# Loading the second head pair's q and k in f32 through ScalarE's DMA queue, with the cast on GpSimd

## The chip, the cores and the metric

The kernel runs on one core of a Trainium2 chip. A core has TensorE (PE, matrix products and transposes), VectorE (DVE), ScalarE (ACT) and GpSimd (POOL), and SyncE (SP), which here only issues transfers. Transfers between the chip's main memory (HBM) and the on-chip SBUF run on 16 DMA engines that all queues share. The metric is the device time of one execution in microseconds (us); the number given for the kernel is the median of several runs.

## What is computed

The reference is a causal attention whose heads are of two kinds, followed by a soft mixture of experts with slots. All inputs and the output are f32.

```python
# q, k, v: (4, 8, 768, 64); retrieval heads see all earlier positions,
# the others only 4 sink positions and a window of 64
scores = q @ k.T / sqrt(64);  scores = where(mask, scores, -1e9)
a = exp(scores - max);        a = a / sum(a)
x = (a @ v)  rearranged to (3072, 512)
# soft mixture of experts: 8 experts, 4 slots each, phi (512, 32)
logits = x @ phi
d = softmax(logits, axis=0);  slot_input = d.T @ x
slot_out[e] = relu(slot_input[e] @ w1[e]) @ w2[e]     # w1 (8,512,1024), w2 (8,1024,512)
c = softmax(logits, axis=1);  out = c @ slot_out      # (3072, 512)
```

## The kernel before, in words

The 32 pairs of batch and head are worked off as 16 head pairs, n = 0 to 15. For one pair the loop (`for n in range(NP)`) does six chunks of scores on TensorE (`scores`, L174), each followed by an exponential on ScalarE (L187) that writes the transposed probabilities `pT` in bf16; a mask multiplication on VectorE (`mask`, L189); and, one pair later, the products with v (`pvmm`, L201) and the division by the row sum (`norm`, L211). q and k must first be transposed: `transposes` (L147) does this on TensorE from the bf16 tile `raws`, and `evac` (L156) copies the result to SBUF, q on VectorE (L165), k on ScalarE (L167). The transposes for a pair are placed within the loop step before it; those for the second pair (n = 1) stand at the end of step 0, behind its sixth chunk.

The order on every engine is the order of the source (`tc.manual_schedule()`); each engine and each queue works its instructions in that order, and waits are put between engines where data or a buffer demands them.

There are three DMA queues in use. GpSimd's queue takes nearly all loads. It reads f32 from HBM and writes bf16 into SBUF, so it casts on the way: `load_four` (L121) brings q and k for four heads, `load_v` (L125) brings v for four heads, `w_load` (L138) and later lines bring the expert weights. In step 0 and 1 of the loop it issues, in this order: q and k of the second four heads, the first expert's w1, the second v, q and k of the third four, the third v, and then weights as they come due. ScalarE's queue takes one thing only: the first pair's q and k, in f32, into the tile `stage` (L264 to L266). From there VectorE casts q (L293) and ScalarE casts k (L294) into the first half of `raws[0]`. SyncE's queue takes a 64-byte input, and the output at the end.

The second pair's q and k are the other half of `raws[0]`. `load_pair(1)` (L270) brings them by GpSimd's queue, as its first two transfers, ahead of an iota (L272) that VectorE needs for the identity matrix and the masks, and of the first v (L274).

Before the loop, TensorE runs 12 matrix products on zeros (`keep_busy`, L285) and then the first pair's transposes. VectorE builds the mask tiles (L295 to L322) between the casts and the first mask multiplication.

The tile `stage` is taken from the pool `ptp`, which has two buffers and serves the probabilities `pT` in turn. The pool `raw` has three buffers of q and k for four heads each.

After the loop, the last weights are loaded, the slots are summed, and the experts are computed: first products L534, second products L573 and `second` (L561, its matrix product on L565). The second products of the last expert are made in two halves, left and right, as their weights arrive; then the output is formed (L589 to L599) and stored.

Of the kernel before, what the change touches and what calls it, by code (L numbers as in the profile page):

```python
# [10 lines left out]
F32 = mybir.dt.float32  # L11
# [27 lines left out]
def kernel(  # L39
# [13 lines left out]
    nc = tc.nc  # L53
    P = 128
    B, H, S, D = q.shape
# [12 lines left out]
    ptp = ent(tc.tile_pool(name="ptp", bufs=2))  # L68
# [6 lines left out]
    def single(shape, dt, name, tag=None):  # L75
        return singles.tile(shape, dt, name=name, tag=tag or name)
# [23 lines left out]
    raws, TT, vf, pT, pv, xb = {}, {}, {}, {}, {}, {}  # L100
# [7 lines left out]
    def features(x, n):  # L108
        if n < 2:
            return x[:, :, :256].rearrange("p i (x g d) -> p i g x d", x=2, g=2)[:, :, n]  # L110
        return x[:, :, 128 * (n % 4):128 * (n % 4) + 128].rearrange("p i (h d) -> p i h d", h=2)

    def load_pair(n, order="qk"):
        for which in order:
            src, z = (q, 0) if which == "q" else (k, 1)
            nc.gpsimd.dma_start(raws[0][:, z, n * S:(n + 1) * S],
                                src[0, 2 * n:2 * n + 2].rearrange("h (p s) d -> (h p) (s d)", s=12))

    def load_four(m):
        b, h = m // 2, 4 * (m % 2)  # L120
        raws[m] = raw.tile([P, 2, 2 * S], BF16, tag="raw", name="raw")  # L121
        for z, src in enumerate((q, k)):
            nc.gpsimd.dma_start(raws[m][:, z], src[b, h:h + 4].rearrange("h (p s) d -> (h p) (s d)", s=24))

    def load_v(m):  # L125
        b, h = m // 2, 4 * (m % 2)
        nc.gpsimd.dma_start(vbs[m % 3].rearrange("p h j d -> p (h j) d")[:, :, :D],  # L127
                            v[b, h:h + 4].rearrange("h (j p) d -> p (h j) d", p=P))
# [9 lines left out]
    def w_load(upto):  # L138
        while wi[0] < min(upto, 2 * NE - 3):
            e = wi[0] % NE  # L140
            dst, src = ((w1s, w1v), (w2s, w2v))[wi[0] // NE]

            for p0, p1 in ((0, 112), (112, 117), (117, 122), (122, 127), (127, P)) if wi[0] == NE else ((0, P),):
                nc.gpsimd.dma_start(dst[e][p0:p1], src[e][p0:p1])  # L144
            wi[0] += 1
# [28 lines left out]
    def scores(n, c):  # L174
        o, ln, parts = CHUNKS[c]
        sc = scp.tile([P, 2, 512], F32, tag="sc", name="sc")
        at = 0
        kT, qT = TT[n // 2, "k"][:, n % 2], TT[n // 2, "q"][:, n % 2]
        for j, i0, cnt in parts:
            for hh in range(2):  # L180
                po = 64 * hh
                nc.tensor.matmul(sc[:, hh, at:at + 128 * cnt], kT[po:po + 64, j * 128:(j + 1) * 128],  # L182
                                 qT[po:po + 64, i0 * 128:(i0 + cnt) * 128], start=True, stop=True)
            at += 128 * cnt
        if c == 0:
            pT[n] = ptp.tile([P, 2, NPT], BF16, tag="pT", name="pT")
        nc.scalar.activation(pT[n][:, :, o:o + ln], sc[:, :, :ln], ACT.Exp, scale=scale)  # L187
# [13 lines left out]
    def pvmm(n, i):  # L201
        if i % 3 == 0:
            pv[n] = pvp.tile([P, 3, 2, 65], F32, tag="pv", name="pv")
        for hh in range(2):
            for j in range(i + 1):
                vv = vb(n) if i - j <= 1 else vf[n]
                o = BLK[j, i]
                nc.tensor.matmul(pv[n][:, i % 3, hh, :], pT[n][:, hh, o:o + 128], vv[:, hh, j, :D + 1],  # L208
                                 start=(j == 0), stop=(j == i))

    def norm(n, half):  # L211
        b, h = n // 4, 2 * (n % 4)
        if h == 0 and half == 0:
            xb[b] = xp.tile([P, 6, DM], BF16, tag="xb", name="xb")
        rs = small.tile([P, 3, 2, 1], F32, tag="rs", name="rs")
        nc.vector.reciprocal(rs, pv[n][:, :, :, 64:65])  # L216
        nc.vector.tensor_mul(  # L217
            features(xb[b][:, 3 * half:3 * half + 3], n),
            pv[n][:, :, :, :64], rs.to_broadcast([P, 3, 2, 64]))
# [10 lines left out]
    def logits_mm(b, dbs):  # L230
        if b not in lgs:
            lgs[b] = trp.tile([P, 256], F32, tag="tr", name="lg")
        for db in dbs:
            for g in range(3):
                nc.tensor.matmul(lgs[b][32 * g:32 * g + 32, :], phi[:, db], xT[:, db, 256 * g:256 * (g + 1)],  # L235
                                 start=(db == 0), stop=(db == 3))

    def logits_exp(b):
        nc.scalar.activation(expT[:, b], lgs[b][:96], ACT.Exp, accum_out=colpart[:, b:b + 1])  # L239
# [21 lines left out]
            nc.vector.tensor_add(slot_acc, slot_acc, sp)  # L261


    stage = ptp.tile([P, 2, S], F32, tag="pT", name="stage")  # L264
    for src, z in ((k, 1), (q, 0)):
        nc.scalar.dma_start(stage[:, z], src[0, 0:2].rearrange("h (p s) d -> (h p) (s d)", s=12))  # L266
    ir32 = is_retrieval.tensor.reshape([H]).bitcast(I32)
    nc.sync.dma_start(ri, bass.AP(tensor=ir32, offset=0, ap=[[0, 1], [1, 2 * H]]))
    raws[0] = raw.tile([P, 2, 2 * S], BF16, tag="raw", name="raw")
    load_pair(1)  # L270
    diff = single([P, 256], F32, "diff", tag="slot_acc")
    nc.gpsimd.iota(diff, pattern=[[1, 256]], base=0, channel_multiplier=-1,  # L272
                   allow_small_or_imprecise_dtypes=True)
    load_v(0)  # L274

    V = nc.vector
    zero = single([P, 512], BF16, "zero")
# [2 lines left out]
    def keep_busy(t, count):  # L280
        for _ in range(count):
            nc.tensor.matmul(t, zero[:, :P], zero, start=True, stop=True)  # L282
# [7 lines left out]
    sk2 = single([P, 1], F32, "sk2")  # L290
    ge = single([P, 256], BF16, "ge", tag="slot_bf")
    grade = single([P, 640], BF16, "grade", tag="expT")
    V.tensor_copy(raws[0][:, 0, :S], stage[:, 0])  # L293
    nc.scalar.copy(raws[0][:, 1, :S], stage[:, 1])  # L294
    V.tensor_single_scalar(ge, diff, 0.0, op=ALU.is_ge)  # L295
    V.tensor_single_scalar(rne, ri.rearrange("p (h c) -> p h c", c=2), 0.0, op=ALU.not_equal)
    V.tensor_tensor(rrow1, rne[:, :, 0], rne[:, :, 1], op=ALU.max)
# [43 lines left out]
    for n in range(NP):  # L341
        if n == 0:
            load_four(1)
            nc.gpsimd.dma_start(w1s[0], w1v[0])
            load_v(1)
        elif n == 1:
            load_four(2)
            load_v(2)
        elif n % 2 == 0 and n < 12:
            load_four(n // 2 + 2)  # L350
        elif n % 2 == 1 and n < 12:
            load_v((n + 3) // 2)
        w_load(1 + 5 * (n + 1) // 8)
        if n == 3:
            for a in range(2):
                for g in range(2):
                    nc.gpsimd.dma_start(phi[64 * g:64 * g + 64, 2 * a:2 * a + 2],
                                        moe_phi.rearrange("(a g x d) s -> a g d x s", a=2, g=2, x=2)[a, g])

        m, x = (1, 0) if n == 1 else (n // 2 + 1, n % 2)  # L360
        turns = 0 < n < NP - 2
        b, r = n // 4 - 1, n % 4
        last = n - 1

        scores(n, 0)
        if n == 0:
            keep_busy(idle, 1)
        if n >= 1:
            for i in range(3):
                pvmm(last, i)  # L370
        if b >= 0 and r == 2:
            logits_mm(b, (0, 1, 2, 3))

        scores(n, 1)
        if n == 0:
            keep_busy(idle, 1)
        if b >= 0 and r == 2:
            logits_exp(b)
        if n >= 1:
            norm(last, 0)  # L380
        if turns:
            evac(m, x, "q", transposes(m, x, "q"))
        mask(n, 0)
        if b >= 0 and r == 3:
            exp_tokens(b)

        scores(n, 2)
        if n == 0:
            keep_busy(idle, 1)
        if n >= 1:  # L390
            pvmm(last, 3)
        if n == 3:
            x_transpose(0)
        if n >= 3:
            x_transpose(n - 2)
        mask(n, 1)

        scores(n, 3)
        if n == 0:
            keep_busy(idle, 1)  # L400
        if turns:
            tk = transposes(m, x, "k")

        scores(n, 4)
        if n == 0:
            keep_busy(idle, 1)
        if turns:
            evac(m, x, "k", tk)
        if n >= 1:
            pvmm(last, 4)  # L410
        mask(n, 2)
        if n:
            vfar(n)

        scores(n, 5)
        if n == 0:
            vfar(0)
        if n >= 1:
            pvmm(last, 5)
            norm(last, 1)  # L420
        if b >= 0 and r == 3:
            dispatch_mm(b)
            slot_sum(b)
        if n < 2:
            for which in ("q", "k"):
                evac(n, 1, which, transposes(n, 1, which))
        if n < 3:
            far_mask(n + 1)
            for h in range(H)[heads(n + 1)]:
                head_mask(h)  # L430
        elif n == 3:
            setup_late()

            expT = single([96, B, 256], BF16, "expT")
            slot_acc = single([P, DM], F32, "slot_acc")
            slot_bf = single([P, DM], BF16, "slot_bf")
# [232 lines left out]
```

## Time and profile before

| What | Value |
|---|---|
| Median of 5 runs | 154.42 us (153.55 to 155.46) |
| Profiled execution, its own time | 154.42 us |
| Its span, first to last instruction | 152.6 us |
| TensorE matmul, busy | 121.5 us (80%) |
| VectorE, busy | 107.2 us (70%) |
| ScalarE, busy | 110.1 us (72%) |
| GpSimd, busy | 35.4 us (23%) |
| GpSimd's DMA queue (q0) | 31,936 packets, 25.86 MB written |
| ScalarE's DMA queue (q10) | 288 packets, 0.79 MB |
| HBM read / written | 52.49 MB / 6.29 MB |

Times in the profile's rows are microseconds from the start of the span, unless marked ns. A row of the timeline gives start, duration, engine, line, operation, what it writes and reads, shapes, and how often; in brackets stands how long the engine had been idle before it and what ended that. In a table of stretches, each row is a stretch of time with its length, the busy time of each engine with its number of instructions, the clock granted to TensorE, the busy share of the DMA engines, and the GB/s that they wrote. A transfer's packets overlap on an engine, so the DMA share can pass 1. GpSimd counts as busy while it issues a transfer[...].

### The profile page before, as it was taken

The numbers are of one execution on the slowest core, as the hardware profiler recorded it, in microseconds if no ns is written. First come the engines' busy times: TensorE is split into PE (matmuls) and PEld (weight loads), VectorE is DVE, ScalarE is ACT, GpSimd is POOL, SyncE is SP. The second block draws the span as 40 slices with busy tenths as digits, with TensorE's granted clock in tenths as the row PEclk, the third lists the DMA queues.
The fourth block names the chain that finished last, engine by engine and source line by source line (L and its number), as shares of the span: only waits on it lengthen the run. The fifth ranks groups of instructions, "written<-read, shape, count | busy, mean of one in ns | idle before, by whom it ended". The sixth has DMA issues, their size and how long they took to land. (4 is left out here: it accounts for less than half of the span.)

```text
span 152.6 us, 4812 instructions
## 1 busy us (share of the span) xinstructions
PE 121.5 (80%) x2119; PEld 74.6 (49%) x2119; DVE 107.2 (70%) x246; ACT 110.1 (72%) x148; POOL 35.4 (23%) x54
## 2 busy tenths in 40 slices
PE   6985979868788989988989989877977999389500
PEld 2433656555555655656556666544626354234200
DVE  1299979998987879979698898678835131549600
ACT  3278888959799899999999999999351131268700
POOL 7972000652116061051036220010240000000000
PEclk9999789999999999999999999999997589956975
DMA  5999999999999999999999999999999999988996
GB/s 172 184 196 224 180 205 187 214 201 186 216 193 224 175 212 221 172 221 204 186 214 205 185 220 213 211 215 219 217 208 221 219 210 191 143 274 345 412 396 222
DMA packets 34886, 33.23 MB, mean 218 GB/s; under 512 B 26147, under 2 KB 30003, under 8 KB 32563
## 3 DMA queue, kind: packets, MB, share of 16 engines
q0 software_dynamic: 31936, 25.86, 107.7%
q1 hardware_dynamic: 2642, 6.29, 10.8%
q10 hardware_dynamic: 288, 0.79, 1.5%
q8 instruction: 16, 0.26, 0.6%
q14 instruction: 4, 0.03, 0.1%
HBM read 52.49 MB, written 6.29 MB: 385 GB/s over the span
## 5 line engine op out<-in xcount | busy, mean ns | idle before, releaser
L187 ACT ACTIVATE pT<-sc 128x1024 bf16<-128x1024 f32 x96 | 82.4, 937 | 7.5 <-PE sc L182 6.5
L182 PE MATMUL sc<-Tq,Tk 64*128 64x256 bf16 (+3 forms) x256 | 35.5, 313 | 11.7 <-ACT pT L187 5.5
L208 PEld LDWEIGHTS <-pT 128*128 128x128 bf16 x672 | 24.5, 98 | 14.0 <-issue 10.6
L199 DVE TENSOR_TENSOR pT<-pT,msk 128x1024 bf16<-128x1024 bf16 (+1 forms) x48 | 29.5, 640 | 1.2 <-ACT pT L187 1.0
L208 PE MATMUL pv<-vb,pT 128*128 128x65 bf16 x352 | 27.1, 194 | 0.3 <-DVE xb L217 0.3
L208 PE MATMUL pv<-vf,pT 128*128 128x65 bf16 x320 | 25.0, 196 | 0.0
L182 PEld LDWEIGHTS <-Tk 64*128 64x128 bf16 x256 | 12.0, 93 | 19.8 <-issue 8.0
L127 POOL DMA_DIRECT2D vb<-in_v_dram x8 | 11.5, 1443 | 42.3 <-PE pv L208 24.4
L165 DVE COPY Tq<-tpq 128x768 bf16<-128x768 bf16 x16 | 15.3, 956 | 6.2 <-PE tpq L153 6.1
L153 PEld LDWEIGHTS <-raw 64*64 64x64 bf16 x768 | 15.2, 111 | 7.1 <-issue 5.2
L217 DVE TENSOR_TENSOR xb<-pv,rs 128x384 bf16<-128x384 f32 x32 | 17.8, 558 | 1.1
L167 ACT COPY Tk<-tpk 128x768 bf16<-128x768 bf16 x16 | 12.7, 796 | 2.7 <-PE tpk L153 2.7
L144 POOL DMA_DIRECT2D w<-in_moe_w_dram x16 | 8.7, 546 | 16.8 <-DMA w<-in_moe_w_dram 10.0
L153 PE MATMUL tpk<-ident,raw 64*64 64x64 bf16 x384 | 9.5, 199 | 1.6 <-DVE Tq L165 1.1
L589 PE MATMUL bank<-slot_out,expR 128*128 128x512 bf16 (+2 forms) x30 | 9.6, 431 | 1.1 <-DVE slot_out L603 0.5
L216 DVE RECIPROCAL rs<-pv 128x6 f32<-128x6 f32 x32 | 6.2, 195 | 5.4 <-PE pv L208 4.6
L225 PE MATMUL tpx<-ident,xb 128*128 128x128 bf16 x96 | 8.1, 219 | 2.3 <-DVE Tq L165 1.3
L226 DVE COPY xT<-tpx 128x768 bf16<-128x768 bf16 (+1 forms) x17 | 8.9, 529 | 1.4 <-PE tpx L225 1.4
L153 PE MATMUL tpq<-ident,raw 64*64 64x64 bf16 x384 | 9.1, 194 | 0.1
L282 PE MATMUL idle<-zero 128*128 128x512 bf16 x20 | 8.1, 534 | 1.2 <-DVE zero L278 1.2
L591 ACT ACTIVATE ot<-bank,rrow 128x512 f32<-128x512 f32 (+2 forms) x11 | 6.7, 640 | 1.1 <-PE bank L589 1.1
L225 PEld LDWEIGHTS <-xb 128*128 128x128 bf16 x96 | 6.0, 97 | 3.1 <-issue 3.0
(94 smaller groups left out, 109.0 us busy)
## 6 DMA issues: line engine op xcount, KB each, us to landing
w<-in_moe_w_dram POOLq DMA_DIRECT2D x14, 1024.0 KB, 16.5
vb<-in_v_dram POOLq DMA_DIRECT2D x8, 384.0 KB, 11.6
out_dram<-ot SPq DMA_DIRECT2D x3, 1024.0 KB, 4.7
raw<-in_q_dram POOLq DMA_DIRECT2D x7, 384.0 KB, 15.9
raw<-in_k_dram POOLq DMA_DIRECT2D x7, 384.0 KB, 17.2
w<-in_moe_w_dram POOLq DMA_DIRECT2D x2, 512.0 KB, 20.6
out_dram<-ot SPq DMA_DIRECT2D x2, 512.0 KB, 6.8
w<-in_moe_w_dram POOLq DMA_DIRECT2D x1, 896.0 KB, 18.9
```

Of the source, the lines that this page charges most:

```text
L127: nc.gpsimd.dma_start(vbs[m % 3].rearrange("p h j d -> p (h j) d")[:, :, :D], v[b, h:h + 4].rearrange("h (j p) d -> p (h j) d", p=P))
L153: nc.tensor.transpose(tp[po, s, :], src[po, 64 * s:64 * s + 64], ident[po, po])
L165: nc.vector.tensor_copy(o, i)
L167: nc.scalar.copy(o, i)
L182: nc.tensor.matmul(sc[:, hh, at:at + 128 * cnt], kT[po:po + 64, j * 128:(j + 1) * 128], qT[po:po + 64, i0 * 128:(i0 + cnt) * 128], start=T ...
L187: nc.scalar.activation(pT[n][:, :, o:o + ln], sc[:, :, :ln], ACT.Exp, scale=scale)
L199: nc.vector.tensor_mul(x, x, m)
L208: nc.tensor.matmul(pv[n][:, i % 3, hh, :], pT[n][:, hh, o:o + 128], vv[:, hh, j, :D + 1], start=(j == 0), stop=(j == i))
L217: nc.vector.tensor_mul(features(xb[b][:, 3 * half:3 * half + 3], n), pv[n][:, :, :, :64], rs.to_broadcast([P, 3, 2, 64]))
L225: nc.tensor.transpose(tp[:, i * 128:(i + 1) * 128], xb[b][:, i, hp * 128:(hp + 1) * 128], ident)
L226: nc.vector.tensor_copy(xT[:, hp, i0 * 128:i1 * 128], tp[:, i0 * 128:i1 * 128])
L589: nc.tensor.matmul(op, er[r], slot_out[:, cs], start=True, stop=True)
```

## The change

The tile `stage` becomes a list of two, one per head pair, and ScalarE's queue loads k and q of both pairs in f32, four transfers in place of two. `load_pair` goes away. GpSimd's queue now begins with the first v, which moves ahead of the iota; the loads behind it keep their order. In step 0 of the loop, behind that step's loads and ahead of those of step 1, GpSimd casts the whole second stage tile (q and k, 128 x 1536 f32) into the second half of `raws[0]`. Both buffers of `ptp` are now taken by stage tiles before the first and second `pT` use them.

```diff
-    def load_pair(n, order="qk"):
-        for which in order:
-            src, z = (q, 0) if which == "q" else (k, 1)
-            nc.gpsimd.dma_start(raws[0][:, z, n * S:(n + 1) * S],
-                                src[0, 2 * n:2 * n + 2].rearrange("h (p s) d -> (h p) (s d)", s=12))
...
-    stage = ptp.tile([P, 2, S], F32, tag="pT", name="stage")
-    for src, z in ((k, 1), (q, 0)):
-        nc.scalar.dma_start(stage[:, z], src[0, 0:2].rearrange("h (p s) d -> (h p) (s d)", s=12))
+
+    stage = [ptp.tile([P, 2, S], F32, tag="pT", name=f"stage{n}") for n in range(2)]
+    for n in range(2):
+        for src, z in ((k, 1), (q, 0)):
+            nc.scalar.dma_start(stage[n][:, z],
+                                src[0, 2 * n:2 * n + 2].rearrange("h (p s) d -> (h p) (s d)", s=12))
...
-    load_pair(1)
+    load_v(0)
     diff = single([P, 256], F32, "diff", tag="slot_acc")
     nc.gpsimd.iota(diff, pattern=[[1, 256]], base=0, channel_multiplier=-1,
                    allow_small_or_imprecise_dtypes=True)
-    load_v(0)
...
-    V.tensor_copy(raws[0][:, 0, :S], stage[:, 0])
-    nc.scalar.copy(raws[0][:, 1, :S], stage[:, 1])
+    V.tensor_copy(raws[0][:, 0, :S], stage[0][:, 0])
+    nc.scalar.copy(raws[0][:, 1, :S], stage[0][:, 1])
...
         w_load(1 + 5 * (n + 1) // 8)
+        if n == 0:
+            nc.gpsimd.tensor_copy(raws[0][:, :, S:], stage[1])
```

## The prediction

> **What bounds the kernel now.** I read the page first: the slices, the DMA queues, then the chain of waits.
>
> ```profile
> span 152.6 us, 4812 instructions
> DMA  5999999999999999999999999999999999988996
> GB/s 172 184 196 224 180 205 187 214 201 186 216 193 224 175 212 221 172 221 204 186 214 205 185 220 213 211 215 219 217 208 221 219 210 191 143 274 345 412 396 222
> q0 software_dynamic: 31936, 25.86, 107.7%
> q10 hardware_dynamic: 288, 0.79, 1.5%
> ```
>
> The DMA engines are busy from the second slice to the end. Nearly all of that is q0, GpSimd's queue, whose transfers read f32 and write bf16; q10 is ScalarE's queue, today only the first pair's q and k. So I looked at whether q0 ever runs empty, and at what the end waits for: the chain of waits, then TensorE's timeline near the end.
>
> ```profile
> 111.40 0.90 POOL w L443
> 112.30 21.44 DMA w<-in_moe_w_dram
> 133.74 0.04 issue
> 133.78 0.64 PE bank L565 x7
> ```
>
> ```profile
> 131.13 0.40 PE L565 MATMUL bank<-w,hT 128*32 128x256 bf16 x8 [1.38 <-DMA w<-in_moe_w_dram]
> ```
>
> The last weights were issued at 112.30 and landed 21.44 us later, at 133.74. That isn't the price of 0.25M elements; it is a backlog. With the DMA view cut to single issues, each transfer on q0 lands one service time after its predecessor: 1 MB of bf16 weights each 4.9 us, a 384 KB v 2.5 us, a 384 KB q or k 1.9 us, and each is issued well before its turn (5 us in the head, 8 or more later). So q0 is one serial line from its first packet to 133.74, and the output follows. TensorE's work is ready 1.38 us before the left half of the last expert's weights. Compute, with ScalarE's exponentials nearly gapless from 16 to 107 us, has that much slack.
>
> Hence two questions: by how much does the line on q0 shift, and does the head of the compute slip by more than 1.38 us?
>
> **The line.** Stretches of the head (last two columns: DMA share, GB/s written):
>
> ```profile
> 1.50:4.00 2.50, 2.50 (x7) 0.91 (x6) 0.35 (x2) 1.58 (x2) 2.41 (x4) 1.00 0.85 297
> 5.00:6.00 1.00, 1.00 (x4) 0.30 (x2) 0.96 (x4) 0.00 (x0) 1.00 (x2) 1.00 1.08 128
> 6.00:9.00 3.00, 2.80 (x59) 1.60 (x57) 1.40 (x4) 0.80 (x1) 3.00 (x5) 1.00 2.19 164
> 9.50:12.00 2.50, 1.84 (x11) 0.79 (x9) 2.39 (x13) 2.50 (x4) 1.18 (x2) 1.00 1.07 210
> ```
>
> GpSimd's issues in the head (start, duration):
>
> ```profile
> 1.24 0.70 POOL L116 DMA_DIRECT2D raw<-in_q_dram  x1 [0.80 <-POOLq L650]
> 2.87 1.47 POOL L127 DMA_DIRECT2D vb<-in_v_dram  x1
> 6.20 1.45 POOL L127 DMA_DIRECT2D vb<-in_v_dram  x1
> 8.67 1.47 POOL L127 DMA_DIRECT2D vb<-in_v_dram  x1
> ```
>
> Removed: the second pair's cast loads. By the DMA view they take 4.9 and 5.3 us from issues at 1.24 and 1.94, so q lands at 6.1 and k at 7.2: 1.1 us each on the line, 2.2 together. v, issued at 2.87, lands 6.9 us later, at 9.7, so it takes 2.5. Between 5 and 6 us the line moves only 128 GB/s where q and k otherwise move 210 (9.5 to 12 us), some 0.4 us lost: v was issued late, and its first packets come after 6 us.
>
> Added: 786 KB f32 on q10. Written width doubles, but what the DMA engines pay for is what is read: q10 moves 402 GB/s between 3 and 4 us, reading as much, while q0 writes 210 and so reads 420. The cast therefore costs the line nothing, and moving the pair saves little: 786 KB / 402 GB/s = 1.96 us against 2.2. They share the same engines, so this is a swap and not an offload. What else can be won is the 0.4 us: four transfers on q10 keep the engines fed to about 6.7 us, and v, now first on GpSimd's queue at 1.24, is ready behind or beside them. Sum: 1.96 − 2.2 − 0.4 = −0.6; as v's longer issue may leave part of the hole, I take −0.5. Ends: −0.2 if the hole stays; −1.1 if v, whose small packets read only 328 GB/s alone (twice 164), moves at the full 402 beside the large ones (786/402 = 1.96 for 2.5, another −0.5).
>
> Everything behind v on q0 keeps its order and shifts by this. GpSimd issues the third quarter's q, k, v and the second weights later, since the cast stands ahead of them: wait to about 7, cast to about 9, so they start near 9.1 instead of 7.62. Their turn on the line only comes after the second v lands (21.6), so 10 us of cover remain; gone, each us of lateness would cost one.
>
> **ScalarE's queue.** Two more issues of 0.38 to 0.46 us move the table load from 1.63 to about 2.5, ending 3.8; the cast of k's first pair, now at 3.70, starts there. SyncE's late issues with several transfers in flight took 1.05 to 1.3 us, so at worst the cast ends near 6.0. TensorE takes the first transposes only at 6.41, behind its keep-busy matmuls: no cost either way.
>
> **The cast on GpSimd.** No row shows one. The nearest: GpSimd's iota, 256 elements in 0.37 us, six times which is 2.2; VectorE's 768-element cast, 0.56 us, twice which is 1.1. I take 2.0 (by the engine's own row), with 1.1 and double the iota, 4.4, as ends. It waits for both halves of the pair, landing between 7.0 (v behind them) and 8.9 (fair sharing): done at 9 to 11. The second pair's transposes come at 12.86. Covered by 2 us or more; at 4.4 from 8.9 it is 0.4 late. The second probability tile, which takes the second stage's buffer, is first written at 15.8: no wait.
>
> **VectorE beside it.** This is the one cost that I do not put at nothing.
>
> ```profile
> 8.92 0.29 DVE L304 TENSOR_TENSOR grade<-grade,ge 128x256 bf16<-128x256 bf16 x1
> 9.25 0.91 DVE L305 COPY grade<-grade 128x128 bf16<-128x128 bf16 x1
> 9.36 0.81 DVE L306 TENSOR_SCALAR sk<-diff 128x1 f32<-128x1 f32 x1
> 28.67 1.15 DVE L321 CAST fmask<-r 128x396 bf16<-128x396 f32 x1
> ```
>
> L305, L306 and this L321 (0.3 to 0.4 elsewhere) end just when an issue of v by GpSimd ends (10.14, 29.65); L304, with two inputs, is not held by the same issue. The Trainium skill ("SBUF — State Buffer", Who interferes with whom) gives a rule against this change: the port pair shared by the two engines is an exclusive lock, and a GpSimd instruction that reads SBUF, as a cast does and a DMA issue here did not, also holds VectorE's instructions with two SBUF inputs. By the rows alone (only one-input copies held), the cast to 9.3 costs nothing, since L305 starts at 9.25. By the rule L303, two inputs, at 8.47, is held to the cast's end: +0.8. Then L305 and L306 no longer meet a v issue (−0.65), but the third v, now at about 10.4 to 11.9, meets the small scalar operations at 10.98: +0.9. The second v, now at about 4.9 to 6.4, can hold the cast L293 of the first q, ready at 5.0, to 6.4 and a little more; its transposes start at 7.01: 0 to +0.3. Rows: about +0.25 in all. Rule: about +1.0. I take the rule, +1.0; ends −0.2, and about 3 with the 4.4 us cast. VectorE is gapless from 7.6 to 20 us and TensorE waits 1.54 for it at 15.35, so the slip goes into the whole loop. At the end work is ready at slip − 1.38 and the weights at −0.5, and the later counts: 1.0 − 1.38 = −0.4 against −0.5. The two come out nearly even, with −0.4 for the sum of all parts.
>
> **The rivals.** *The line shifts and the slip fits the slack* (0.60): −0.4. Profiled execution 152.6 → 152.2; its own time was 154.42, 1.8 above its span and equal to the median of the runs, so 154.0. *v overlaps fully and nothing holds VectorE* (0.12): −1.1, 153.3. Against it: v is slow by its packet count, not only by what is read. *The hole stays or another wait eats the gain* (0.12): −0.1, 154.3. For it: the first packets of q0 came 2.8 us after the first issue, and v's issue takes twice as long. *The cast holds VectorE* (0.16), the slower side: in the stretch 7 to 13 us a cast of 4 us or a chain of held instructions delays the second pair's scores. It makes the kernel slower than before once the slip passes 1.38 us; at 3 it gives +1.6, 156.0; at 3.5, 156.5. For it: VectorE has no gap there. Against it: ScalarE's own cast of 768 elements needs only 0.83 us, and 4 us would be nearly five of those. That the change does not do what it says is excluded by q10, which would show twice the packets.
>
> **The numbers.** 154.0 is the likeliest. From full overlap with a quiet median (153.0) to a slip near 2.6 us (155.6) should hold 8 in 10; the five runs themselves spread from 153.55 to 155.46. One per cent, 1.54 us, is about what a measurement can tell from no change. Faster by more: 0.06, only full overlap with luck. Slower by more: 0.16, the last rival. Same: 0.78.
>
> **What would show it.** q10 with 1.57 MB in 576 packets; GB/s of 300 or more until about 6.5 us and no 128 there; v landing at 9.2 instead of 9.7, and the last weights near 133.2; TensorE's wait before L565 shrunk from 1.38 us to some 0 to 0.7; the span's end following the last weights by the same 18.9 us. It would be wrong if the cast row shows over 3 us, if VectorE shows instructions ending at its end with the second pair's first scores beyond 17 us, or if q0 shows a gap.

## The result and the profile after

| What | Before | After |
|---|---|---|
| Median of the runs | 154.76 us (80 runs, 153.37 to 156.07) | 155.91 us (43 runs, 154.29 to 156.92) |
| Ratio after / before | | 1.0069, 95% interval 1.0053 to 1.0085 |
| Profiled execution, its own time | 154.42 us | 154.71 us |
| Last weights landed | 133.74 us | 134.74 us |
| Last exponential of the loop ended | 107.63 us | 109.95 us |

The change makes the kernel slower by 0.7%, where I had forecast 0.4 us less. (The 154.42 us of the forecast were the median of five runs of before; over 80 runs it is 154.76.) The profiled execution of after was one of the fastest of its runs; two more of the same kernel (below) lie nearer to its median. The page after, in its first lines, the slices and the queues:

```profile
span 152.9 us, 4817 instructions
DMA  5999999999999999999999999999999999979995
GB/s 162 259 191 219 197 193 184 210 207 186 222 189 227 179 199 219 186 216 199 186 224 196 189 207 219 221 212 208 221 223 208 214 223 187 162 239 416 411 393 190
q0 software_dynamic: 31648, 25.46, 105.8%
q10 hardware_dynamic: 576, 1.57, 3.4%
```

The transfers are those of the change: q10 moves 1.57 MB in 576 packets. The line is still busy to the last weights. The chain of waits, and TensorE's row ahead of the left half of the last expert's weights:

```profile
113.73 0.90 POOL w L441
114.62 20.12 DMA w<-in_moe_w_dram
134.74 0.04 issue
134.78 0.43 PE bank L563 x8
```

```profile
132.13 0.40 PE L563 MATMUL bank<-w,hT 128*32 128x256 bf16 x8 [0.80 <-DMA w<-in_moe_w_dram]
```

The end still follows the weights, and TensorE still waits for them, 0.80 us in place of 1.38. But they land 1.0 us later than before; I had them 0.5 us earlier. Where the line lost that is seen in the same stretches as before (the last column is what the DMA engines wrote, in GB/s):

```profile
1.50:4.00 2.50, 2.50 (x7) 0.91 (x6) 0.35 (x2) 1.39 (x2) 2.42 (x4) 1.00 0.84 269
5.00:6.00 1.00, 0.77 (x26) 0.45 (x24) 0.65 (x1) 0.19 (x1) 1.00 (x1) 1.00 0.98 222
6.00:9.00 3.00, 2.10 (x35) 1.09 (x37) 2.70 (x8) 0.81 (x2) 0.27 (x1) 1.00 1.76 222
9.50:12.00 2.50, 1.79 (x9) 0.74 (x8) 2.46 (x10) 2.50 (x4) 2.50 (x4) 1.00 1.32 209
```

The 128 of the stretch from 5 to 6 us is gone, and 222 stands there. But before, these GB/s were cast loads, which read twice what they write (the 52.49 MB read from HBM are nearly twice q0's 25.86 plus q10's 0.79), so 256 GB/s read; after, they are f32, read and written alike. Counted in bytes read, by the packets of the trace that had started, the loads had read 2041 KB by 8 us before and 1797 KB after, 3656 and 3337 KB by 12 us. At some 400 GB/s the 320 KB are 0.8 us of line. About half of them, 160 KB, are lost from 4 to 6 us, where the loads read 329 GB/s before and 248 after. The landings are later too: the first v at 11.38 us (before 9.74), q and k behind it at 13.19 and 15.05 (11.52, 13.38), the first weights at 19.95 (19.14), the last at 134.74 (133.74).

GpSimd's rows in the head of after:

```profile
1.25 1.56 POOL L121 DMA_DIRECT2D vb<-in_v_dram  x1 [0.80 <-POOLq L648]
4.80 1.46 POOL L121 DMA_DIRECT2D vb<-in_v_dram  x1
9.13 1.46 POOL L351 CAST raw<-stage 128x1536 bf16<-128x1536 f32 x1 [2.87 <-DMA stage<-in_q_dram]
11.69 1.64 POOL L121 DMA_DIRECT2D vb<-in_v_dram  x1
```

The cast takes 1.46 us and is done at 10.59, 2 us ahead of the transposes that need it. VectorE beside it, first the row of before that L304 is compared with (there it is L308), then after:

```profile
10.39 0.48 DVE L308 SCALAR_TENSOR_TENSOR grade<-ge,sk,grade 128x256 bf16<-128x256 bf16 x1
```

```profile
5.35 1.30 DVE L289 CAST raw<-stage 128x768 bf16<-128x768 f32 x1 [1.70 <-DMA stage<-in_q_dram]
8.96 0.20 DVE L301 COPY grade<-grade 128x128 bf16<-128x128 bf16 x1
9.44 1.43 DVE L304 SCALAR_TENSOR_TENSOR grade<-ge,sk,grade 128x256 bf16<-128x256 bf16 x1
12.19 1.17 DVE L318 CAST fmask<-r 128x132 bf16<-128x132 f32 x1
```

L304, with two inputs, took 0.48 us before and 1.43 here, and ends 0.28 us behind GpSimd's cast. L289 (0.56 before) is held by the second issue of v, L318 (0.22) by the third; L301 (0.91 before, as L305) no longer is. The holds are of the kind foreseen, but here they cancel: the row behind L304 starts at 10.80 us, and at 10.79 before. The 0.95 us that the cast adds to L304 replace some 0.66 by which L305 and L306 were held before, and VectorE came to this work 0.28 us earlier (8.19 us for 8.47).

### The profile page after: what moved, and what is told of

It reads as the page before. It is cut to its first block, busy times and chain, and to the rows that moved or that the text cites. A ratio compares the mean times of both kernels' runs of the same rounds, so it can differ in the third digit from the quotient of the medians.

```text
span 152.9 us, 4817 instructions
## 1 busy us (share of the span) xinstructions
PE 118.4 (77%) x2119; PEld 74.2 (49%) x2119; DVE 107.9 (71%) x246; ACT 110.1 (72%) x148; POOL 35.6 (23%) x53
## 3 DMA queue, kind: packets, MB, share of 16 engines
q10 hardware_dynamic: 576, 1.57, 3.4%
HBM read 52.49 MB, written 6.29 MB: 384 GB/s over the span
## 5 line engine op out<-in xcount | busy, mean ns | idle before, releaser
L181 ACT ACTIVATE pT<-sc 128x1024 bf16<-128x1024 f32 x96 | 82.6, 935 | 11.1 <-PE sc L176 9.8
L202 PEld LDWEIGHTS <-pT 128*128 128x128 bf16 x672 | 25.0, 99 | 14.4 <-issue 10.8
L587 PE MATMUL bank<-slot_out,expR 128*128 128x512 bf16 (+2 forms) x30 | 7.6, 330 | 1.8 <-DVE slot_out L601 0.5
L278 PE MATMUL idle<-zero 128*128 128x512 bf16 x20 | 6.9, 462 | 1.2 <-DVE zero L274 1.2
L165 DVE TENSOR_TENSOR vf<-vb,fmask 128x528 bf16<-128x528 bf16 x16 | 6.9, 428 | 0.0
## 6 DMA issues: line engine op xcount, KB each, us to landing
w<-in_moe_w_dram POOLq DMA_DIRECT2D x2, 512.0 KB, 19.2
```

The source lines that it names most:

```text
L587: nc.tensor.matmul(op, er[r], slot_out[:, cs], start=True, stop=True)
```

## The experiments

**Does the order on GpSimd's queue matter?** First, v behind the next q and k:

```diff
-    load_v(0)
+    load_four(1)
     diff = single(...); nc.gpsimd.iota(diff, ...)
+    load_v(0)
```

> The changed kernel, with q and k of the second four heads first on GpSimd's queue and the first v behind the iota. Theory A (v's small packets, queued beside the f32 loads, slow the DMA engines in the head): ScalarE's queue moves about 400 GB/s from 2.5 to 5.5 us as it did for the first pair, the second stage lands before 7 us, the last weights land near 133.2, ratio to the kernel before 0.995 to 0.999. Theory B (four f32 transfers on ScalarE's queue are slow whatever lies behind them): that queue again falls below 300 GB/s from 3.5 us, last weights near 134.7, ratio 1.005 to 1.008. Theory C (the cast on GpSimd costs the time): ratio 1.005 to 1.008 too, though the queue is fast.

Median 154.76 us, ratio 1.0019 (0.9992 to 1.0046). With large cast packets beside the f32 ones the engines read 3109 KB by 10 us (before 2808, after 2505), some 395 GB/s, and the last weights land at 133.65. The loss of after is gone, although the four f32 transfers and the cast are still there. Theory A's other marks did not come: sharing the engines with q and k, the second pair lands at 9.43 and 10.87 us, not before 7, and the lead at 10 us is spent again by 16 us, where v runs late and alone.

Then v first, in the kernel before and with nothing else changed:

```diff
     raws[0] = raw.tile(...)
+    load_v(0)
     load_pair(1)
     diff = single(...); nc.gpsimd.iota(diff, ...)
-    load_v(0)
```

> The kernel before, with only the order on GpSimd's queue changed: the first v ahead of the second pair's q and k. Theory A: v meets only the tail of the first pair's f32 loads, some loss, last weights 0.2 to 0.6 us later than before, ratio 1.001 to 1.004. Theory B and C: nothing lost, ratio 0.999 to 1.001. If the whole slowdown comes from v standing first (its long issue leaving the queue without packets until 5.7 us), the ratio is 1.006 or more here as well.

Median 154.36 us, ratio 0.9981 (0.996 to 1.0002); v lands at 7.48 us, the last weights at 133.40. v first is no harm by itself, where theory A had expected some. So neither part alone is the loss: it needs v first and the four f32 transfers together.

**The cast.** Added alone to the kernel before, into weights that are overwritten later:

```diff
+        if n == 0:
+            nc.gpsimd.tensor_copy(w2s[4][:, 0:3, :], stage...)
```

> The kernel before, with an additional GpSimd cast of the first stage tile (128 x 1536 f32 to bf16) into a weight tile that is not yet loaded, at the place of the change's cast; nothing uses its result. Theory A and B: cast of 1.5 us near 7.7 us, last weights where they were, ratio 0.999 to 1.001. Theory C: the cast holds VectorE and delays GpSimd's issues, ratio 1.004 to 1.008.

154.89 us, ratio 1.0019 (0.9995 to 1.0043). In its trace the first v lands at 10.79 us and the last weights at 134.61, but q had already landed late (6.70 for 6.12), before this cast ran. So the head differs between executions by up to a microsecond even where the program is the same; single traces must be read with that in mind. In this trace the cast did delay work: VectorE's L296, a small one-input instruction, took 1.47 us (0.15 before) and ended with the cast, a longer hold of L295 stood ahead of it, and the second pair's scores began at 17.26 us for 15.35. TensorE then came to the last weights at 134.66 without waiting. The other direction, cut down in the kernel after:

```diff
+    V.memset(raws[0][:, :, S + 16:], 0.25)
...
-            nc.gpsimd.tensor_copy(raws[0][:, :, S:], stage[1])
+            nc.gpsimd.tensor_copy(raws[0][:, :, S:S + 16], stage[1][:, :, :16])
```

> The changed kernel, with the GpSimd cast cut to 16 of 768 columns of q and k; the rest of the tile is filled by a VectorE memset at 1.1 us, where VectorE is idle. The second pair's q and k are left out, so that pair's output is not the reference's; every load and every wait stays. Theory A2: the line is as in the changed kernel, ratio 1.005 to 1.008. Theory C (the cast on GpSimd costs a part): ratio 1.000 to 1.004.

It leaves most of the second pair's q and k at a constant. 155.70 us, ratio 1.0072 (1.0051 to 1.0092), last weights at 134.57: with next to no cast, and the two-input instruction back at 0.49 us, the loss is whole. The cast is not the loss.

**Which wait ends last in after?** Two more executions of the kernel after:

> The changed kernel unaltered, a second profiled execution, since the first was among its faster ones (154.71 against a median of 155.91). Theory A (the head's DMA loss makes q of the third four heads land after 24.1 us, where TensorE needs it, and the slip of the compute loop uses up the slack before the last weights): that landing at 24.5 or later, exponentials ending after 109.5, and in an execution near the median TensorE's wait for the last weights gone or below 0.5 us. Theory D (the line of loads alone decides): last weights at 135.5 or later in an execution near the median, and TensorE still waits 0.5 us or more for them.

> The same, a third profiled execution, to see how much the head differs from one to the next. Theory A and D as for the second look; the landing of the first v between 10.5 and 12.

Their own times are 156.44 and 156.03 us. TensorE's rows ahead of the left half of the last weights, of the second and the third execution:

```profile
132.75 0.40 PE L563 MATMUL bank<-w,hT 128*32 128x256 bf16 x8 [2.03 <-DMA w<-in_moe_w_dram]
132.38 0.40 PE L563 MATMUL bank<-w,hT 128*32 128x256 bf16 x8 [1.81 <-DMA w<-in_moe_w_dram]
```

The last weights land at 135.36 and 134.99, a little earlier than theory D had them; TensorE waits for the left half and again about 0.4 us for the right. So the line decides the end in all three executions of after, and by more than the first trace shows: the three executions of after average 135.03, the four of kernels with the head of before (before, the cast alone, and two controls below) 133.97. That is 1.06 us, against 1.15 between the medians. From these weights to the end of the span it takes 18.2, 19.2 and 19.3 us in the three, 18.9 before: the first trace shows the loss smaller than it usually is.

The loop also ends later in after, since q of the third four heads, 1 us late, now comes after its need (24.74 us; it is used at 24.1). To see whether that costs, the first weights were loaded behind the third v, which brings this q forward, in after and in before:

```diff
-            nc.gpsimd.dma_start(w1s[0], w1v[0])
...
             load_v(2)
+            nc.gpsimd.dma_start(w1s[0], w1v[0])
```

> The changed kernel, with the first expert's w1 (1 MB on the line, not used before the end) issued behind the third v instead of ahead of the second: q of the third four heads lands 4.9 us earlier, near 19.9. The total on the line stays. Theory A: TensorE no longer waits for that q, exponentials end near 107, ratio to the kernel before 0.996 to 1.002. Theory D: the last weights land as late as in the changed kernel, ratio 1.005 to 1.008.

> The kernel before, with the same w1 issued behind the third v. Theory A: in the executions in which q of the third four heads landed after 24.1 us something is won, ratio 0.993 to 0.999. Theory D: the line ends as before, ratio 0.999 to 1.001.

This q then lands at 19.14 us and is not waited for, yet after stays at 155.89 us, ratio 1.009 (1.0067 to 1.0113); before stays at 154.98, 1.0014 (0.9994 to 1.0035). That alone does not clear the wait, since the trace of after with w1 late is slow by another way. VectorE was held twice (L300 took 1.43 us beside the cast, L306 1.14 beside an issue of v), the second pair's scores began at 17.07 us, the loop ended at 111.47, and TensorE came to the right half of the last weights (landed 134.83) without waiting:

```profile
135.31 0.40 PE L563 MATMUL bank<-w,hT 128*32 128x256 bf16 x8
```

That the wait at 24 us does not set the end rests on the three traces of after itself, in which TensorE stands waiting for the weights in spite of it.

**Is it v's small packets?** v in packets of 768 bytes written in place of 128, in after and in before; its rows then lie in other places, so the first four heads' output is not the reference's:

```diff
+        if m == 0:
+            nc.gpsimd.dma_start(vbs[0].rearrange("p h j d -> p h (j d)")[:, :, :6 * D],
+                                v[b, h:h + 4].rearrange("h (p j) d -> p h (j d)", p=P))
+            return
```

> The changed kernel, with the first v alone loaded in runs of 1536 read bytes (six neighbouring rows per partition) instead of 256; the same bytes, but the rows stand in other places, so the first four heads of the output are not the reference's. A memset of the tile's tail is added on VectorE while it is idle. Theory A2 (v's small packets, active beside the second pair's f32 loads, hold all traffic near 300 GB/s): the head reads near 400 GB/s, the last weights land before 133.5, ratio to the kernel before 0.993 to 0.998. Rival (any cast load first on GpSimd's queue beside four f32 transfers does it): traffic again near 300 GB/s from 3.5 us, ratio 1.003 to 1.008.

> The kernel before with the same edit of the first v, the control: with the same difference in the output. Both theories: v takes 2.0 us on the line instead of 2.5, ratio 0.995 to 0.999. Theory A2 expects the previous run within 0.003 of this one or below it; the rival 0.005 or more above it.

1.0047 (1.0023 to 1.0071) and 0.9971 (0.9952 to 0.999): between the two 0.0076, as large as the whole loss. That speaks against v's small packets as the cause; 768 bytes are still fewer than the 3072 of the four-head q and k.

**Are the four f32 transfers slow by themselves, and does a second queue help?** The cast moved ahead of GpSimd's first load, so that the f32 transfers run alone:

```diff
-    load_v(0)
     diff = single(...); nc.gpsimd.iota(diff, ...)
+    nc.gpsimd.tensor_copy(raws[0][:, :, S:], stage[1])
+    load_v(0)
```

> The changed kernel, with the GpSimd cast moved ahead of GpSimd's first load, so that ScalarE's four f32 transfers meet no other load until they have landed. Theory B (the third and fourth transfer on ScalarE's queue are slow by themselves): below 300 GB/s from 3.5 us and the fourth landing at 7 us or later. Theory E (they are slow only while a cast load is in work on GpSimd's queue): 400 GB/s to the end, the fourth landing before 6.4 us. In both the line starts late: last weights some 2 to 4 us later than in the changed kernel.

And the second pair on SyncE's queue, with everything else as in after:

```diff
-            nc.scalar.dma_start(stage[n][:, z],
+            (nc.scalar, nc.sync)[n].dma_start(stage[n][:, z],
```

> The changed kernel, with the second pair's two f32 transfers on SyncE's queue, beside the first pair's on ScalarE's. Theory B (one queue's later transfers are slow): the two queues move 400 GB/s together, second pair landed before 6.5 us, ratio 0.997 to 1.003. Theory E: traffic near 300 GB/s from the moment the first v is in work, near 3.5 us, ratio 1.004 to 1.009.

The stretch from 4 to 6 us tells the three kernels apart. It holds almost nothing but f32 packets (the first v packets come at 5.7 us in after, at 6.1 with the second queue, at 11.1 with the f32 transfers alone). After, then the f32 transfers alone, then with the second queue:

```profile
4.00:6.00 2.00, 1.77 (x30) 0.84 (x28) 0.65 (x1) 0.91 (x2) 2.00 (x3) 1.00 1.05 252
```

```profile
4.00:6.00 2.00, 2.00 (x6) 0.61 (x4) 0.99 (x4) 0.78 (x1) 0.00 (x0) 1.00 0.99 373
```

```profile
4.00:6.00 2.00, 2.00 (x6) 0.61 (x4) 0.00 (x0) 0.66 (x1) 2.00 (x3) 1.00 1.02 396
```

Alone the four transfers move 373 GB/s and land at 3.92, 4.85, 6.35 and 7.33 us (after: 3.76, 5.33, 7.86, 8.99). That is far above theory B's 300 GB/s but short of theory E's 400 and 6.4 us. The kernel is of course late for lack of loads, 161.05 us. With the second queue they move 396 GB/s though the same v is issued at the same time (1.25 us), against theory E, and the last weights land at 133.71, as before; this is one trace. That kernel still takes 155.50 us, 1.003 (1.0005 to 1.0056), by another way: the first pair now shares with the second and lands at 5.32 and 7.14 us, and at the end TensorE comes to the weights at 134.64 without having waited.

**What happens in the line.** The trace records 16 ends for each transfer, which I take as one for each DMA engine; it doesn't say which engine an end belongs to. This table, counted from the trace, gives the first and the last of the 16 ends of the first v; the time between the two is called the lag below. It also gives how many packets that started between 4 and 7 us were held, that is, took over 0.4 us, where a 3 KB f32 packet takes 0.12 and a cast one of q or k 0.13 to 0.25.

| Execution | First end of v | Last end | Held packets | Last weights |
|---|---|---|---|---|
| before | 9.24 us | 9.74 us | 6, cast | 133.74 us |
| before, w1 late | 9.15 | 10.18 | 9, cast | 133.97 |
| before, large v packets | 8.81 | 9.40 | 9, cast, and 1 of v | 133.56 |
| v first alone | 7.14 | 7.48 | 0 | 133.40 |
| v first alone, again | 7.12 | 8.00 | 2, cast | 134.13 |
| q and k, then v | 12.97 | 13.39 | 1, cast | 133.65 |
| second queue | 9.16 | 9.71 | 0 | 133.71 |
| cast alone | 9.21 | 10.79 | 13, cast | 134.61 |
| after | 9.21 | 11.38 | 15, f32 | 134.74 |
| after, second execution | 9.21 | 11.52 | 8, f32 | 135.36 |
| after, third execution | 9.26 | 10.99 | 14, f32 | 134.99 |
| after, w1 late | 9.20 | 11.05 | 11, f32 | 134.83 |
| after, tiny cast | 9.44 | 10.91 | 12, f32 | 134.57 |
| after, large v packets | 9.04 | 10.87 | 11, f32, and 3 of v | 134.73 |

The first end of v is no later in after than before; the last is, by 1.6 us. In after 15 f32 packets were held for 0.4 to 1.6 us, 13.6 us in sum. Spread evenly over the 16 engines, that would be 0.85 us, about what the line lost. But the held packets do not give the lag by their number: the second execution of after has the largest lag, 2.3 us, with 8 of them (5.5 us in sum), and before with large v packets has 10 and a lag of 0.6.

The kernel before has held packets too, and there they are not f32 and not of another queue: they are the second pair's own cast packets, which start between 4.2 and 5.7 us while v stands next behind them on GpSimd's queue. In the cast-alone execution 13 of them go with a lag of 1.58 us and late weights, so the kernel before can fall into this as well; after was in it in all three executions. With v first, before's packets are nearly free of it (0 and 2).

The lag lasts: the next q ends between 10.99 and 13.19 us. Over sixteen executions (all but the three in which GpSimd's loads wait for the cast or ScalarE issues the second pair late) the last weights lie near 133.2 us plus 0.9 times the lag at v (correlation 0.93). That is a relation, not yet a cause. Nor does the lag itself arrive at the end: it grows in every trace, before from 0.50 us at v to 2.99 at the last weights, in after from 2.17 to 3.06, and there the first of the 16 ends is as much later as the last (131.68 for 130.75). What stays is the lost amount: after had read 320 KB less than before at 12 us, 250 at 20, 360 at 60, 330 at 80 and 310 at 120.

**What holds the packets?** v issued later, behind seven iotas, so that it should not run beside the f32 transfers:

```diff
-    load_v(0)
     diff = single(...); nc.gpsimd.iota(diff, ...)
+    for i in range(6):
+        nc.gpsimd.iota(w2s[4][:, i % 2, :256], ...)
+    load_v(0)
```

> The kernel after, with the iota for VectorE and six more iotas of the same size (into weights that are overwritten later) ahead of the first v on GpSimd's queue, so that v is issued at about 3.8 us and its packets should begin at about 6 to 6.5, when the four f32 transfers are nearly done; nothing else changes. New reading of the traces: the 16 DMA engines report each transfer's end one by one, and in the kernel after the earliest engine ends the first v at 9.21 us, as before (9.24), while the latest ends it at 11.38 (before 9.74); single engines fall behind between 4.5 and 8 us and never catch up. Theory F (engines that work off v's cast beside the f32 transfers fall behind): without the overlap the four f32 transfers land as when alone (about 3.8, 4.8, 6.3, 7.3), the 16 engines end v within 0.3 to 0.8 us, v lands at 9.0 to 9.8, the last weights at 133.2 to 133.8, ratio 0.997 to 1.002. Theory G (it is the depth of ScalarE's queue, or just v before q and k on GpSimd's queue, and not the overlap): spread of 1.5 us or more, last weights at 134.5 or later, ratio 1.004 or more.

Theory F fell. 155.83 us, ratio 1.0084 (1.0051 to 1.0117), v's ends 9.47 to 11.13 us, 15 held packets, last weights at 135.15. v was issued at 2.93 us, not 3.8, and its first packet comes at 6.4; nevertheless the f32 transfers slow down from 4 us:

```profile
4.00:6.00 2.00, 2.00 (x6) 0.60 (x4) 0.86 (x4) 0.72 (x1) 2.00 (x4) 1.00 0.97 230
```

230 GB/s, with no packet of v on the way. So it is not v's packets beside the f32 ones. Left were GpSimd's issues in that time (theory H), and a v that has been issued and waits (theory I). So v at 1.25 us as in after, and the next issue only at 5.91 us; and, in a second kernel, only behind the cast:

```diff
     load_v(0)
     diff = single(...); nc.gpsimd.iota(diff, ...)
+    for i in range(9):
+        nc.gpsimd.iota(w2s[4][:, i % 2, :256], ...)
```

> The kernel after, with nine iotas (into weights that are overwritten later) between the first v and GpSimd's further issues, so that v is issued at 1.25 us as in the kernel after but the next issue comes at about 6.0 instead of 3.18. In the traces single packets of ScalarE's f32 transfers take 0.4 to 2.1 us instead of 0.12, nearly all of them between 4.1 and 5.9 us; with v issued late and no v packet before 6.0 they are still there, and with no GpSimd issue in that time there is one. Theory H (packets are held where GpSimd writes the descriptors of other transfers at that time): few packets over 0.4 us from 4 to 6 us, the 16 engines end the first v within 0.8 us, it lands at 9.0 to 9.8 us, last weights at 133.2 to 133.9, ratio 0.997 to 1.002. Theory I (the v that is ready behind the f32 transfers holds them, whoever issues what): held packets as in the kernel after, spread 1.5 us or more, last weights at 134.5 or later, ratio 1.004 or more.

```diff
     load_v(0)
     diff = single(...); nc.gpsimd.iota(diff, ...)
+    nc.gpsimd.tensor_copy(raws[0][:, :, S:], stage[1])
...
-        if n == 0:
-            nc.gpsimd.tensor_copy(raws[0][:, :, S:], stage[1])
```

> The kernel after with GpSimd's cast moved ahead of all its issues but the first v: v is issued at 1.25 us, and nothing else until the second pair has landed and is cast. Theory H: the four f32 transfers land at about 3.8, 4.8, 6.3 to 7.5 and 7.3 to 8.5 us with few packets over 0.4 us, v's spread under 0.8 us and its landing at 9.0 to 9.8; the next loads are issued only at about 9 us or later, so the line has a gap of one or two us behind v and the last weights come at 135 to 136.5. Theory I: spread 1.5 us or more, second pair's q at 8.5 to 9.2, v at 10.9 to 11.5, last weights 135.5 to 137.5.

The first shows 12 held packets, v's ends from 9.39 to 10.81 us and the last weights at 135.05. Its ratio, 1.0025 (0.9995 to 1.0056), tells little, as the medians (155.73 and 154.69) stand 0.7% apart; I go by the trace, which shows theory I's marks but for a spread of 1.42 us. The second has no GpSimd issue at all between 2.8 and 10.7 us, and still:

```profile
4.00:6.00 2.00, 2.00 (x6) 0.61 (x4) 0.99 (x4) 0.72 (x1) 0.00 (x0) 1.00 0.98 261
```

261 GB/s, 12 held packets, ends from 9.34 to 11.48 us (159.05 us in all, since the later loads come late). GpSimd's further issues are not it. The only difference to the f32 transfers alone, at 373, is the v that has been issued ahead of the cast. An issued v does not always do it, however: with q and k ahead of it on GpSimd's queue (the first experiment) v is issued at 2.87 us, and the loads read 392 GB/s from 4 to 6 us. It seems that v must be the next load of its queue.

Last, the same transfers with the roles turned: ScalarE issues the second pair behind its cast of k, so that v is under way first.

```diff
-    for n in range(2):
+    def load_stage(n):
...
+    load_stage(0)
...
     nc.scalar.copy(raws[0][:, 1, :S], stage[0][:, 1])
+    load_stage(1)
```

> The kernel after, with the second pair's two f32 transfers issued by ScalarE behind its cast of the first k (about 4.7 us) instead of right behind the first pair's; v is issued at 1.25 us as in the kernel after, and so runs from 4.05 us on as in the two variants with v first, with no f32 transfer beside it until about 6. Theory I (large f32 packets are held while a v stands ready behind them; a v that already flows is no harm): few packets over 0.4 us from 4 to 7 us, v lands at 7.5 to 8.5, the 16 engines end it within 0.9 us, the second pair lands at about 9 to 10, last weights at 133.4 to 134.2, ratio 0.997 to 1.002. Theory J (v and f32 transfers on two queues harm each other in whatever order): v at 9 or later, spread of 1.4 us or more, last weights at 134.5 or later, ratio 1.004 or more.

Only a part of theory I's marks came true. ScalarE issued at 3.87 us, the line read 1997, 2811 and 3658 KB by 8, 10 and 12 us, which is before's amount, and no packet was held between 4 and 6.9 us. But v's 16 ends lie between 7.16 and 9.04 us, a lag of 1.88 where I had expected 0.9 at most, without held packets. The f32 pair shared the engines with v, q, k and w1 of GpSimd's queue, landed at 11.30 and 16.43 us, and the second pair's scores and with them the whole loop came late (its last exponential ends at 113.49 us): 157.87 us, 1.0208 (1.0142 to 1.0274). The time says nothing on the line here. The packets are not held once v flows first, but a lag can arise without them.

**A version that beats both.** v first without the f32 pair had the smallest lag, and was measured again:

> The kernel before with the first v ahead of the second pair's q and k on GpSimd's queue (still cast loads), for a narrower interval, as it had the earliest last weights of all (133.40 us) and the smallest spread of the 16 engines at the first v (0.34 us). Theory F: two small f32 transfers on ScalarE's queue are done by 4.8 us, before v's packets come in number, so again a spread under 0.7 us, last weights at 133.3 to 133.7, ratio 0.996 to 1.000. Theory G: as v stands ahead of q and k here too, a spread over 1 us in some executions, and a ratio of 1.000 to 1.003.

Median 154.15 us, ratio 0.9967 (0.9948 to 0.9986). With the first run's 0.9981 this is a small gain, 0.2 to 0.3%, from the reordering alone; only the second interval lies clear of 1. Its chain of waits:

```profile
111.49 0.89 POOL w L443
112.39 21.74 DMA w<-in_moe_w_dram
134.13 0.04 issue
134.17 0.64 PE bank L565 x7
```

This execution was one with some lag (0.88 us at v, 134.13), between the marks of the two theories; the first run's had 0.34 and 133.40. Of the two executions the one with the smaller lag ended its weights earlier, by 0.73 us.

## Why the prediction was wrong, step by step

- *q0 is one serial line, and its last weights set the end.* Right in all three executions of after: TensorE waits for both halves. In three variants (second queue, cast alone, after with w1 late) compute came later than the weights.
- *The line shifts by 1.96 − 2.2 − 0.4.* This step failed. I priced the f32 pair at the rate that q10 had between 3 and 4 us (402 GB/s), and v beside it at worst at its own rate, so that the mixture could cost no more than the one after the other. Measured, the f32 transfers run at 252 GB/s from 4 to 6 us once v is issued, against 373 without it, and the last weights come 1.0 us later instead of 0.5 earlier. The 0.4 us of the hole were misread as well. I took it for lack of work, v being issued late; but the second pair's packets still start until 6.7 us, and six of them, from 5.0 to 5.7 us, were held for 0.45 to 0.87 us. The hole was a mild case of the same loss, and the change made it worse: 256 GB/s read between 5 and 6 us became 222.
- *ScalarE's two more issues cost nothing.* Right: its cast of k begins at 3.89 us, for 3.70 before.
- *The cast takes 2.0 us and ends at 9 to 11.* It takes 1.46 us and ends at 10.59 as foreseen; the kernel with hardly any cast is as slow as after.
- *VectorE is held by the cast and the slip is 1.0 us.* The rule of the Trainium skill ("SBUF — State Buffer", Who interferes with whom) held: the two-input L304 took 1.43 us for 0.48. The slip did not come in the trace of after: the second pair's first scores stand at 15.35 us there as before. (In single traces of variants it came, at 17.07 and 17.26 us.) I had taken off the 0.65 us of the old hold, but then added 0.9 for the third v's issue, and that came at 11.69 us, behind the small operations that I thought it would meet; L318, which it did hold, delayed nothing. So neither of the two nearly equal terms that made my forecast, slip and line, came out.
- *10 us of cover for the loads behind the cast.* Right: issued at 10.5 us for a turn after 22.46. What I overlooked is q of the third four heads, which had only 0.6 us to its use; it became late, and the three traces of after, where TensorE waits for the last weights all the same, show that this does not set the end.
- *The rivals.* The slower one put the loss in VectorE beyond a slip of 1.38 us. The loss came from the line itself, which none of them had as longer than before. The mark that I named, the last weights near 133.2, was the right place to look: they landed at 134.74.

What the runs show: the loss needs the f32 pair on ScalarE's queue together with a v that has been issued as the next load of GpSimd's queue, and in the first trace of after half of the lost bytes are missing from 4 to 6 us, where the f32 transfers of eight such traces move 230 to 287 GB/s for 373 alone. It is neither the cast, nor v's packets beside the f32 ones, nor GpSimd's other issues, nor the late q; v's packet size was tested only up to 768 bytes.

Not settled is why packets are held while the next load of GpSimd's queue, v, moves none yet, be they of another queue or, in the kernel before, of its own; why two queues with the same load are free of it, in the one trace that there is; and how much of the lost line the held packets make. The traces show no state of the engines that would tell.

## What to carry to other kernels

Count bytes read, not written, when a cast load is swapped for an f32 load on another queue; the GB/s row of a profile counts what is written, and the swap then looks like a gain. Where a serial line of transfers sets the end, a loss in its first microseconds can stay to the end: here 0.8 us were lost by 12 us, and the last weights were 1.0 us late. A stretch in which a line moves little is not always short of work: look at single packets before counting it as a gain. And before moving a load to another queue, try the order of the queue that it leaves: v first, alone, gave 0.4 and 0.65 us between the medians, about what the whole change was meant to bring.

## What the hardware showed that was not expected

Single 3 KB packets took up to 2.1 us where most take 0.12, with the next transfer of another queue only issued and not yet moving. The lag between the 16 ends of a transfer did not shrink: in after the 2.2 us at the first v were 2.2 us at the next q and k too, and 3.1 at the last weights. The time from a v's issue to its first packet was 2.8 us in the repeat of v first (1.25 to 4.06), 2.3 us with nothing else moving (8.87 to 11.13), and 4.4 us in after (1.25 to 5.68). GpSimd's cast of 128 x 1536 f32 elements took 1.46 us, which is 0.95 ns for each of the 1536, faster than its iota (0.37 us for 256) had led me to think.
